# Batch 0 of a three-block kernel: the low part of transposed P by a matmul, normalization and the low part of q on POOL

## The chip, the cores and the metric

One core of a Trainium2 chip runs the whole program. The metric is device time in microseconds for one execution; the time before is the median of three runs. The engines are PE (matmul), DVE (vector), ACT (scalar), POOL (GpSimd) and SP, which here only issues transfers. Each engine works through its own instructions in order.

## The reference

Three blocks follow one another: attention that keeps only scores near the row's maximum, a gated feed-forward block, and a block with a two-dimensional Fourier transform and a second feed-forward part. The change touches the attention of the first of four batches.

```
q, k, v: (4, 8, 576, 64);  x: (4, 576, 512)
scores = q @ k.T / 8
keep   = scores >= rowmax - tau
attn   = exp(scores - rowmax) where kept, else 0
attn   = attn / (rowsum + 1e-9)
x      = attn @ v                      # heads side by side: 512
xk, xr = mixes of x with the row before it
x      = sigmoid(xr @ w_r) * (relu(xk @ w_k)**2 @ w_v)
u      = x + real(fft2(x))
out    = u + relu(layernorm(u) @ w_ch1) @ w_ch2
```

## The kernel before

All matmuls are to be nearly exact in fp32, but run on operands of type fp32r, which hold fewer bits. So each operand is split into a high part (a copy into fp32r, on ACT) and a low part (the value less the high part), and the products are added up in PSUM. Much of the work of DVE, ACT and POOL is this splitting.

Attention runs over 16 pairs of heads, 4 for each batch, and 9 steps for each pair: steps 0 to 3 and 5 to 8 take 128 rows of one head each, step 4 the 64 rows that remain of both heads. A step goes like this:

- `emit_scores` (line 212, and 226 for step 4): PE multiplies q with the high and low part of k, into PSUM tile "s".
- `emit_max` (252): DVE takes the row maximum; `emit_th` the threshold.
- `emit_exp` (263): ACT takes the exponential into SBUF tile "e" ("em" for step 4).
- `emit_select` (267): DVE zeroes what lies below the threshold and sums the rows; lines 626 and 630 make the reciprocal.
- the normalization: POOL multiplies the rows by it (`emit_norm`, 273), or ACT does (636), as the mask NA0 says step by step for batch 0.
- two steps later `emit_T` (320): PE transposes four 128 x 128 blocks into PSUM tile "t" (two buffers), a fifth one (340) for every second tile.
- its `out`: the transposed P is split into a high and a low part, tile "pt". With the mask SO0 set, ACT copies "t" to SBUF (331) and to the high part (332), and POOL subtracts (333). Otherwise ACT makes the high part and DVE subtracts (305, 306).
- `emit_av` (387, 389): PE multiplies with v, some steps later.

The heads' q and k are loaded by SP into one tile, "rawqk", of a pool with one buffer that v uses too. `conv_k` makes the high part of k on ACT (150) and the low part on POOL (151); `conv_q` makes the high part of q on ACT (157) and the low part on DVE (167), which scales and subtracts in one instruction. These conversions are emitted one pair ahead.

While batch 0 is in work, `weight_pieces` also converts weights for the feed-forward block, 20 pieces of 512 columns, with three DVE instructions on integers (67, 68, 69), a copy on ACT (72) and a subtraction on POOL (73). When all four pairs of a batch are done, the feed-forward block for it starts (line 413 and on), between the attention steps of the next batch. After attention follow the rest of the feed-forward block, the Fourier transform and the mixer.

The order of instructions on each engine is not written by hand: a scheduler puts them in order by priorities from the table `P` and by the times that it expects. The mask bits are the step's place in the pair: 239 is all steps but 4 and 8, 254 is steps 1 to 7. `pi < NPAIR` is batch 0.

Of the kernel before, what the change touches and what calls it, by code (L numbers as in the profile page):

```python
# [9 lines left out]
F32 = mybir.dt.float32  # L10
F32R = mybir.dt.float32r
I32 = mybir.dt.int32
ALU = mybir.AluOpType
AF = mybir.ActivationFunctionType
# [6 lines left out]
HS = S // 2  # L21
NPAIR = H // 2
P = dict(PRI=100, SR=1.0, CR=2, ORD=0, PF=0, CB=0, XT=0, XL=0, K2=0, FE=0, FE3=0, MU=0, WP=256, C1=2, RB=4, BB=2, FT=4, A0=[7, 8], A1=[11, 12], B0=[7, 8], B1=[11, 12], PT4=1, OR0='', XH=0, SP0=0, CA=1.48, CN=2.22, QS=1, pF=100, pM=100, pN=100, pT=100, pO=100, pE=100, pS=100, pA=0, pX=0, NA=0, LT=2, WS=3, WR=1, CC=3.0, BN=2, OR='FATXOESBI', TM=8, SO=0, SO0=0, AO=0, AO0=0, QS0=0, XD=0, TH=0, SM=0, SM0=0, N0=34, qF=100, qM=100, qN=100, qT=100, qO=100, qE=100, qS=100, qA=100, qX=30, RQ=[0,0,0,0,0,0,0,0], XN=0, QN=36, AVR=0, LX=2, WD=0, WP2=512, E3=1, NA0=0, W0=0, XD2=0, PO=0, WP1=512, IN=[0,1,2,2,4,5,6,7])
P.update({'pX': 100, 'CR': 3, 'pA': 100, 'OR': 'FTBXOAESI', 'PF': 300, 'pE': 0, 'pO': 500, 'QS': 2, 'WS': 0, 'FE3': 2, 'pF': 0, 'A0': [7, 9], 'C1': 3, 'BN': 2, 'K2': 0, 'WR': 0.9, 'FT': 2, 'MU': 0, 'SR': 0.6, 'XT': 0, 'SO0': 239, 'XL': 3, 'QS0': 2, 'FE': 2, 'CB': 2, 'AO0': 8, 'IN': [0, 0, 2, 2, 4, 5, 6, 6], 'pN': 30, 'pM': 0, 'A1': [11, 12], 'AVR': 1, 'NA0': 254, 'N0': 30, 'PT4': 0, 'WD': 1, 'qN': 0, 'qS': 500, 'qT': 150, 'QN': 37, 'qE': 0, 'qO': 30, 'B0': [7, 10], 'qX': 60, 'qM': 500, 'E3': 1, 'WP1': 512, 'qF': 300, 'OR0': 'FTBXEOASI', 'B1': [10, 13], 'TH': 4, 'AO': 4, 'qA': 30, 'pS': 300, 'SO': 16, 'RQ': [0, 0, 0, 0, 0, 0, 0, 0]})
PRI = P['PRI']


# [1 line left out]
def tile_kernel(ctx: ExitStack, tc: tile.TileContext, a):  # L29
    nc = tc.nc  # L30
    pe, dve, act, pool, sp = nc.tensor, nc.vector, nc.scalar, nc.gpsimd, nc.sync
# [8 lines left out]
    ident = const.tile([128, 128], F32, name="ident")  # L40
    small = const.tile([128, 46], F32, name="small")
    mus, cons, stats = small[:, 0:16], small[:, 16:19], small[:, 19:46]
# [111 lines left out]
    def conv_q(pi, j):  # L154
        raw, kh, kl = heads[pi, j]
        q = at.tile([128, 640], F32R, tag="q", bufs=3, name="q")
        act.activation(q, raw[:, 0:640], AF.Copy, scale=cons[:, 0:1])
        ql, x = q[64:128], raw[64:128, 0:640]
        qs = P['QS' if pi >= NPAIR else 'QS0'] if pi + j else 2
        if qs == 0:  # L160
            pool.tensor_scalar(x, x, cons[64:128, 0:1], 1.0, op0=ALU.mult, op1=ALU.mult)
            pool.tensor_tensor(ql, x, ql.bitcast(F32), op=ALU.subtract)
        elif qs == 1:
            dve.tensor_scalar(x, x, cons[64:128, 0:1], None, op0=ALU.mult)
            pool.tensor_tensor(ql, x, ql.bitcast(F32), op=ALU.subtract)
        else:
            dve.scalar_tensor_tensor(ql, x, cons[64:128, 0:1], ql.bitcast(F32), op0=ALU.mult, op1=ALU.subtract)  # L167
        heads[pi, j] = (q, kh, kl)
# [25 lines left out]
    def step_of(n):  # L194
        pi, s = divmod(n, 9)
        return pi, ORDER[s]
# [93 lines left out]
    def unit(pi, j, half):  # L290
        if (pi, j, half) not in ptu:
            m = 4 * pi + 2 * half + j
            if P['PT4'] and m % 4 == 3 and m < 4 * NPAIR - 2:
                ptu[pi, j, half] = stage.tile([128, 2, 4, HS], F32R, tag="pt", name="pt4")
            else:
                ptu[pi, j, half] = at.tile([128, 2, 4, HS], F32R, tag="pt", bufs=3, name="pt")
        return ptu[pi, j, half]

    def rem_unit(pi, half):
        if (pi, half) not in ptr:  # L300
            ptr[pi, half] = at.tile([128, 2, HS], F32R, tag="ptr", bufs=2, name="ptr")
        return ptr[pi, half]

    def split_out(hi, lo, src):
        act.activation(hi, src, AF.Copy)  # L305
        dve.tensor_tensor(lo, src, hi.bitcast(F32), op=ALU.subtract)  # L306

    def emit_T(n):
        if not 0 <= n < NSTEP:
            return []  # L310
        pi, tl = step_of(n)
        if tl is None:
            return emit_Tmix(pi, 0)
        j, i = tl
        e = et[pi, i]
        o = 640 if j else 0
        half, sl = i // 2, slice(128 * (i % 2), 128 * (i % 2) + 128)
        t = pst.tile([128, 4, 128], F32, tag="t", name="t")
        for k in range(4):
            pe.transpose(t[:, k, :], e[:, o + 128 * k:o + 128 * (k + 1)], ident)  # L320

        def out():
            u = unit(pi, j, half)
            hi, lo = u[:, 0, :, sl], u[:, 1, :, sl]
            if pi < NPAIR and P['SP0'] >> (n % 9) & 1:
                act.activation(hi, t, AF.Copy)
                pe.matmul(t.rearrange("p k x -> p (k x)"), nid, hi, start=False, stop=True, skip_group_check=True)
                act.activation(lo, t, AF.Copy)
            elif P['SO' if pi >= NPAIR else 'SO0'] >> (n % 9) & 1:
                f = e[:, o:o + 512].rearrange("p (k x) -> p k x", k=4)  # L330
                act.activation(f, t, AF.Copy)
                act.activation(hi, t, AF.Copy)
                pool.tensor_tensor(lo, f, hi.bitcast(F32), op=ALU.subtract)
            else:
                split_out(hi, lo, t)

        todo = [out]
        if j == 1:
            t2 = pst.tile([128, 128], F32, tag="t", name="t2")
            pe.transpose(t2, e[:, 512:640], ident)  # L340

            def out2():
                r = rem_unit(pi, half)
                split_out(r[:, 0, sl], r[:, 1, sl], t2)

            todo.append(out2)
        return todo

    def emit_Tmix(pi, half):
        e = em[pi * 9 + 4]  # L350
        t = pst.tile([128, 4, 2, 2, 32], F32, tag="t", name="tm")
        for k in range(4):
            pe.transpose(t[:, k].rearrange("p a b c -> p (a b c)"), e[:, 128 * k:128 * (k + 1)], ident)
        sl = slice(256, HS)

        def out():
            for j in range(2):
                u = unit(pi, j, half)
                split_out(u[:, 0, :, sl], u[:, 1, :, sl], t[:, :, j, half, :])

        def out2():
            t2 = pst.tile([128, 32], F32, tag="t", name="tm2")
            for j in range(2):
                c = 64 * j + 32 * half
                pe.matmul(t2[64 * j:64 * j + 64], e[:, 512:576], ident[:, c:c + 32], start=True, stop=True)
            r = rem_unit(pi, half)
            split_out(r[:, 0, sl], r[:, 1, sl], t2)

        return [out, out2]
# [195 lines left out]
    dve.tensor_scalar(cons[:, 1:2], tau, -1.0, 0.0, op0=ALU.mult, op1=ALU.min)  # L565
    conv_k(0, 0)
    conv_q(0, 0)
    load_head(0, 1)
    sp.dma_start(ident, a["ident"])
    sp.dma_start(mus[:, 0:4], a["mu_k"])  # L570
    sp.dma_start(mus[:, 4:8], a["mu_r"])
    dve.tensor_scalar(mus[:, 8:16], mus[:, 0:8], -1.0, 1.0, op0=ALU.mult, op1=ALU.add)
    conv_k(0, 1)
    conv_q(0, 1)
    load_v(0)
    conv_v(0)
# [18 lines left out]
    for n in range(P['LX']):  # L595
# [3 lines left out]
    state = dict(stream=None, credit=0.0, w=0.0, s=P['LX'] + 1, m=P['LX'], e=P['LX'])  # L599
    IN = (  # L600
        (load_head, 1, (0,)), (conv_k, 1, (0,)), (conv_q, 1, (0,)), (load_v, 0, ()), (conv_v, 0, ()),
        (load_head, 1, (1,)), (conv_k, 1, (1,)), (conv_q, 1, (1,)),
    )
# [47 lines left out]
    def do_T(n, pi, s):  # L651
        with hp('pT'):
            outs_of[n] = emit_T(n - P['LT'])
# [554 lines left out]
```

## Time and profile before

| what | value |
|---|---|
| median of 3 runs | 1136.56 us (1135.72 to 1139.6) |
| the profiled execution, its own time | 1139.89 us |
| its span in the trace | 1138.1 us |
| busy PE / DVE / ACT / POOL | 1038.4 / 806.7 / 588.9 / 483.8 us |
| mean granted share of the PE clock | 0.969 |

The busy times are over the whole span, in which the first stage (attention of batch 0) is a small part; the rows below are taken from that stage. "A <- B" means that instruction A stood idle until B released it. Matmuls overlap each other in the pipeline, so a busy PE is not PE at its peak.

### The profile page before, as it was taken

To read this page: it belongs to the slowest core of one execution; us is meant where nothing else is said; L and a number is where in the kernel's file an instruction comes from. 1 tells how busy PE (TensorE), PEld (TensorE's weight loads), DVE (VectorE), ACT (ScalarE), POOL (GpSimd) and SP (SyncE) were. 2 spreads that over 40 slices of the span, in tenths; PEclk is the share of its full clock that TensorE was granted. 3 is DMA by queue.
4 is the path that set the end of the run, shared out by engine and by line. 5 is a ranking of instruction groups with operands and counts; after the bars stand their busy time and mean duration, and the time that the engine had idled before them with its cause. 6 is when DMAs were issued, how large, how long until landed. Compare 5 with 4: busy or idle time off the path is not lost.

```text
span 1138.1 us, 19981 instructions
## 1 busy us (share of the span) xinstructions
PE 1038.4 (91%) x7109; PEld 960.0 (84%) x7109; DVE 806.7 (71%) x2093; ACT 588.9 (52%) x1396; POOL 483.8 (43%) x633
## 2 busy tenths in 40 slices
PE   4566769999999999999999997999999999999998
PEld 3555649999988999889988986889999999999997
DVE  7999889889889798897865677975553959322222
ACT  5787777768586685866736564433331212111111
POOL 4556576746467364673634253530001636100000
PEclk9888789999999999999999998999999999999999
DMA  5333321101112011121016255663442546223231
GB/s 171 111 119 96 98 73 56 48 30 54 55 56 76 30 47 56 56 76 32 24 65 159 93 162 178 199 205 120 153 143 90 185 158 190 98 93 109 77 111 56
DMA packets 40395, 114.07 MB, mean 100 GB/s; under 512 B 6191, under 2 KB 6612, under 8 KB 40296
## 3 DMA queue, kind: packets, MB, share of 16 engines
q1 hardware_dynamic: 27200, 74.57, 20.4%
q0 software_dynamic: 10400, 33.50, 9.1%
q10 hardware_dynamic: 2696, 4.73, 1.2%
q8 instruction: 56, 0.92, 0.3%
q14 instruction: 43, 0.35, 0.1%
HBM read 84.45 MB, written 28.32 MB: 99 GB/s over the span
## 4 chain that ended last, share of the span: by engine, by line
PE 65%; DVE 16%; ACT 7%; DMA 6%; issue 4%; POOL 2%; SPq 0%; DVEq 0%; ACTq 0%; POOLq 0%
PE c1ps L969 6%; PE c1ps L971 6%; PE c1ps L970 6%; PE c2ps L984 6%; PE c2ps L982 6%; PE c2ps L983 6%; PE av L387 3%; PE s L212 3%; DVE q L167 3%; DMA rawqk<-in_qk 2%; PE t L320 2%; DVE small L252 2%; PE kps L413 2%; DVE e L267 2%; PE kps L415 2%
## 5 line engine op out<-in xcount | busy, mean ns | idle before, releaser
L975 DVE SCALAR_TENSOR_TENSOR hl<-c1ps,hh 128x256 fp32r<-128x256 f32 x144 | 60.4, 421 | 161.2 <-ACT hh L974 160.6
L974 ACT ACTIVATE hh<-c1ps 128x256 fp32r<-128x256 f32 x144 | 54.3, 379 | 205.7 <-PE c1ps L971 205.6
L252 DVE TENSOR_REDUCE small<-s 128x1 f32<-128x576 f32 x144 | 107.3, 750 | 15.7 <-PE s L212 14.7
L1007 POOL DMA_DIRECT2D ud<-u x54 | 29.5, 546 | 194.2 <-DVE u L1006 138.4
L267 DVE SCALAR_TENSOR_TENSOR e<-s,small,e 128x576 f32<-128x576 f32 x128 | 102.4, 811 | 7.3 <-ACT e L263 5.6
L273 POOL TENSOR_SCALAR e<-e,small 128x576 f32<-128x576 f32 x104 | 82.3, 797 | 46.4 <-DVE small L630 35.4
L263 ACT ACTIVATE e<-s,small 128x576 f32<-128x576 f32 x128 | 92.6, 742 | 14.4 <-DVE small L252 13.4
L212 PE MATMUL s<-kh,q 128*128 128x288 f32 x256 | 65.4, 340 | 29.8 <-DVE q L167 13.7
L320 PE MATMUL t<-ident,e 128*128 128x128 f32 x512 | 81.2, 290 | 7.9 <-DVE ptr L306 2.9
L969 PE MATMUL c1ps<-ut,cA 128*128 128x256 f32 x288 | 82.5, 286 | 2.2 <-ACT ut L960 1.5
L970 PE MATMUL c1ps<-ut,cA 128*128 128x256 f32 x288 | 82.0, 285 | 0.0
L523 PE MATMUL vps<-k,wv 128*128 128x288 f32 x256 | 76.7, 302 | 5.4 <-DVE tg L529 4.6
L971 PE MATMUL c1ps<-ut,cA 128*128 128x256 f32 x288 | 81.6, 283 | 0.0
L971 PE MATMUL c1ps<-ut,cB 128*128 128x256 f32 x288 | 81.0, 281 | 0.0
L969 PE MATMUL c1ps<-ut,cB 128*128 128x256 f32 x288 | 80.9, 281 | 0.0
L970 PE MATMUL c1ps<-ut,cB 128*128 128x256 f32 x288 | 80.7, 280 | 0.0
L485 POOL TENSOR_TENSOR k<-relu,k 128x288 fp32r<-128x288 f32 x64 | 54.1, 847 | 60.6 <-ACT k L483 59.7
L306 DVE TENSOR_TENSOR pt<-t,pt 128x512 fp32r<-128x512 f32 x100 | 67.8, 684 | 16.4 <-ACT pt L305 15.7
L413 PE MATMUL kps<-xh,wk 128*128 128x288 f32 x256 | 78.3, 306 | 0.8 <-ACT relu L470 0.4
L387 PE MATMUL av<-pt,v 128*128 128x288 f32 x408 | 71.3, 308 | 8.1 <-ACT pt L305 3.8
L414 PE MATMUL kps<-xl,wk 128*128 128x288 f32 x256 | 75.8, 296 | 0.0
L415 PE MATMUL kps<-xh,wk 128*128 128x288 f32 x256 | 75.6, 296 | 0.0
(240 smaller groups left out, 3552.8 us busy)
## 6 DMA issues: line engine op xcount, KB each, us to landing
rawqk<-in_qk SPq DMA_DIRECT2D x32, 608.0 KB
u<-ud SPq DMA_DIRECT2D x36, 512.0 KB
wraw<-in_w_ch POOLq DMA_DIRECT2D x64, 256.0 KB, 3.3
ud<-u POOLq DMA_DIRECT2D x54, 256.0 KB, 2.5
rawv<-in_v SPq DMA_DIRECT2D x16, 288.0 KB
un<-ud SPq DMA_DIRECT2D x18, 256.0 KB
out<-u SPq DMA_DIRECT2D x18, 256.0 KB
wraw<-in_w_k SPq DMA_DIRECT2D x8, 512.0 KB
```

What stands on the lines that cost most here:

```text
L212: pe.matmul(ps[:, h, 0:HS], q[:, c:c + 128], kk[:, h * HS:(h + 1) * HS], start=(x == 0), stop=(x == 1),)
L252: dve.tensor_reduce(st[:, 0:1], sps[n][:, :, 0:HS], axis=AX.XY, op=ALU.max, negate=True)
L263: act.activation(two(eview(n)), sps[n][:, :, 0:HS], AF.Exp, bias=st[:, 0:1])
L267: dve.scalar_tensor_tensor(e, sps[n][:, :, 0:HS], st[:, 1:2], e, op0=ALU.is_ge, op1=ALU.mult, accum_out=st[:, 2:3])
L273: pool.tensor_scalar(e, e, st[:, 2:3], 1.0, op0=ALU.mult, op1=ALU.mult)
L320: pe.transpose(t[:, k, :], e[:, o + 128 * k:o + 128 * (k + 1)], ident)
L387: pe.matmul(ps, v[:, 4 * j + k, :], u[:, x, k, :], start=(k == 0 and x == 0), stop=False)
L413: pe.matmul(ps, wh, x[0][:, k, :], start=(k == 0), stop=False)
L415: pe.matmul(ps, wl, x[0][:, k, :], start=False, stop=(k == nk - 1))
L969: pe.matmul(ps, wh, ut[0][:, k, :], start=(k == 0), stop=False)
L970: pe.matmul(ps, wh, ut[1][:, k, :], start=False, stop=False)
L971: pe.matmul(ps, wl, ut[0][:, k, :], start=False, stop=(k == 3))
```

## The change

For batch 0 alone, three switches are set anew. SP0 takes the steps that SO0 had: ACT makes the high part, PE adds minus the high part to the tile "t" in PSUM (a matmul with minus the identity), and ACT copies what is left as the low part. NA0 = 0 gives all normalizations to POOL. QS0 = 3 lets ACT scale q in place and POOL subtract, for all heads of batch 0 but the first. The tile `nid` with minus the identity is made once on ACT. For all batches, the four transposes of a tile are written as one group of matmuls, with the start flag on the first and the stop flag on the last.

```diff
-P.update({... 'SO0': 239, ... 'QS0': 2, ... 'NA0': 254, ...})
+P.update({... 'SP0': 239, 'SO0': 0, ... 'QS0': 3, ... 'NA0': 0, ...})
...
         if qs == 0:
             pool.tensor_scalar(x, x, cons[64:128, 0:1], 1.0, op0=ALU.mult, op1=ALU.mult)
             pool.tensor_tensor(ql, x, ql.bitcast(F32), op=ALU.subtract)
+        elif qs == 3:
+            act.activation(x, x, AF.Copy, scale=cons[64:128, 0:1])
+            pool.tensor_tensor(ql, x, ql.bitcast(F32), op=ALU.subtract)
...
         for k in range(4):
-            pe.transpose(t[:, k, :], e[:, o + 128 * k:o + 128 * (k + 1)], ident)
+            pe.matmul(
+                t[:, k, :], e[:, o + 128 * k:o + 128 * (k + 1)], ident,
+                start=(k == 0), stop=(k == 3), is_transpose=True, skip_group_check=True,
+            )
```

The two branches of `out` that the masks choose between were in the kernel before:

```python
if pi < NPAIR and P['SP0'] >> (n % 9) & 1:
    act.activation(hi, t, AF.Copy)
    pe.matmul(t.rearrange("p k x -> p (k x)"), nid, hi, start=False, stop=True, skip_group_check=True)
    act.activation(lo, t, AF.Copy)
elif P['SO' if pi >= NPAIR else 'SO0'] >> (n % 9) & 1:
    f = e[:, o:o + 512].rearrange("p (k x) -> p k x", k=4)
    act.activation(f, t, AF.Copy)
    act.activation(hi, t, AF.Copy)
    pool.tensor_tensor(lo, f, hi.bitcast(F32), op=ALU.subtract)
```

## Rows read from the trace of the kernel before

**Rows 1.** Stretches: us; length, busy PE, PEld, DVE, ACT, POOL; PEclk, DMA, GB/s.

```profile
20.00:60.00 40.00, 25.38 (x128) 22.64 (x128) 38.00 (x98) 30.84 (x60) 22.49 (x19) 0.87 0.37 112
60.00:100.00 40.00, 27.05 (x157) 23.45 (x156) 37.49 (x91) 31.33 (x67) 24.68 (x22) 0.79 0.38 114
100.00:140.00 40.00, 26.64 (x148) 23.52 (x146) 35.28 (x94) 31.36 (x65) 25.51 (x23) 0.79 0.34 103
140.00:175.00 35.00, 23.09 (x123) 19.42 (x122) 30.81 (x74) 24.28 (x52) 26.85 (x28) 0.80 0.20 62
175.00:220.00 45.00, 43.02 (x328) 41.23 (x327) 40.02 (x118) 36.96 (x89) 29.99 (x40) 1.00 0.16 50
220.00:600.00 380.00, 365.09 (x2786) 350.78 (x2786) 318.50 (x895) 258.30 (x618) 213.31 (x286) 1.00 0.17 53
```

**Rows 2.** DVE's waits on other compute engines, 0 to 175 us: total, times, longest.

```profile
...
DVE small L252 <- PE s L212: 2.9, 6, 0.9
...
```

**Rows 3.** The chain that ended last, 20 to 175 us: its head, by line.

```profile
by line: issue 13.1%; DVE small L252 10.7%; DVE e L267 8.9%; DVE wbits L68 6.8%; DVE wbits L69 6.0%; DVE wbits L67 5.9%; PE avs L387 5.3%; DVE q L167 5.0%; PE s L212 3.4%; PE t L320 2.9%; DMA wraw<-in_w_v 2.7%; PE s L226 2.4%; POOL kl L151 
...
```

**Rows 4.** DVE's groups, 0 to 175 us: busy us, mean ns, idle before.

```profile
...
L68 DVE SCALAR_TENSOR_TENSOR wbits<-wraw,wbits 128x512 int32<-128x512 int32 x20 | 19.7, 986 | 0.1
L69 DVE SCALAR_TENSOR_TENSOR wbits<-wraw,wbits 128x512 int32<-128x512 int32 x20 | 19.0, 948 | 0.1
L67 DVE TENSOR_SCALAR wbits<-wraw 128x512 int32<-128x512 int32 x20 | 15.4, 771 | 2.4 <-POOL wr L73 0.8 <-POOL wk L73 0.8 <-DMA wraw<-in_w_v 0.6
...
```

**Rows 5.** Single lines, 0 to 175 us: ns min/median/max, first and last start.

```profile
L67 DVE TENSOR_SCALAR wbits<-wraw x20: 406/427/1500, 7.6 to 163.0; 128x512 int32<-128x512 int32 x20
...
L68 DVE SCALAR_TENSOR_TENSOR wbits<-wraw,wbits x20: 675/989/1878, 8.0 to 163.8; 128x512 int32<-128x512 int32 x20
...
L69 DVE SCALAR_TENSOR_TENSOR wbits<-wraw,wbits x20: 672/692/1634, 8.8 to 165.6; 128x512 int32<-128x512 int32 x20
...
L252 DVE TENSOR_REDUCE small<-s x41: 730/747/759, 9.4 to 174.3; 128x1 f32<-128x576 f32 x41
...
```

**Rows 6.** Stretches of line 167 alone: length, busy DVE; PEclk, DMA, GB/s.

```profile
10.00:115.00 105.00, 8.07 (x7) 0.85 0.38 116
115.00:175.00 60.00, 3.89 (x3) 0.77 0.26 77
...
```

**Rows 7.** ACT's groups, 0 to 175 us.

```profile
...
L636 ACT ACTIVATE e<-e,small 128x576 f32<-128x576 f32 x24 | 18.4, 774 | 6.1 <-DVE small L630 5.9
L332 ACT ACTIVATE pt<-t 128x512 fp32r<-128x512 f32 x28 | 16.7, 598 | 0.0
...
L157 ACT ACTIVATE q<-rawqk,small 128x640 fp32r<-128x640 f32 x11 | 9.0, 818 | 0.0
...
```

**Rows 8.** POOL's groups, 0 to 175 us.

```profile
L333 POOL TENSOR_TENSOR pt<-e,pt 128x512 fp32r<-128x512 f32 x28 | 39.1, 1397 | 22.4 <-ACT pt L332 14.4 <-PE t L320 5.6 <-issue 2.3
L151 POOL TENSOR_TENSOR kl<-rawqk,kh 128x576 fp32r<-128x576 f32 x10 | 15.9, 1593 | 7.6 <-ACT kh L150 4.2 <-PE tm L365 3.4
...
L273 POOL TENSOR_SCALAR e<-e,small 128x576 f32<-128x576 f32 x11 | 10.3, 939 | 6.9 <-DVE small L630 5.8 <-DVE ptr L306 1.1
...
```

**Rows 9.** Timeline at the start: start us, us, instruction, idle before it.

```profile
15.05 0.85 PE L212 MATMUL s<-kh,q 128*128 128x288 f32 x2 [6.13 <-DVE q L167]
```

**Rows 10.** What SP's queue waited for, 0 to 175 us.

```profile
...
SPq L143 <- DVE q L167: 25.6, 6, 7.1
...
```

**Rows 11.** What engines waited for, 20 to 175 us.

```profile
...
ACT kh L150 <- DMA rawqk<-in_qk: 3.8, 5, 1.8
...
```

**Rows 12.** Single lines: 982 over the span, 387 from 20 to 175 us.

```profile
L982 PE MATMUL c2ps<-cA,hh x144: 389/389/501, 703.2 to 1035.3; 128*128 128x512 f32 x144
...
L387 PE MATMUL avs<-pt,v x104: 290/442/608, 40.9 to 151.5; 128*128 128x288 f32 x104
...
```

**Rows 13.** PE's waits, 20 to 175 us.

```profile
...
PE tm L353 <- ACT pt L332: 7.3, 4, 3.0
...
PE t L340 <- ACT pt L332: 3.8, 4, 2.0
...
```

More of the change, by code (lines that the diff above doesn't have):

```diff
@@ L23 @@
 P = dict(PRI=100, SR=1.0, CR=2, ORD=0, PF=0, CB=0, XT=0, XL=0, K2=0, FE=0, FE3=0, MU=0, WP=256, C1=2, RB=4, BB=2, FT=4, A0=[7, 8], A1=[11, 12], B0=[7, 8], B1=[11, 12], PT4=1, OR0='', XH=0, SP0=0, CA=1.48, CN=2.22, QS=1, pF=100, pM=100, pN=100, pT=100, pO=100, pE=100, pS=100, pA=0, pX=0, NA=0, LT=2, WS=3, WR=1, CC=3.0, BN=2, OR='FATXOESBI', TM=8, SO=0, SO0=0, AO=0, AO0=0, QS0=0, XD=0, TH=0, SM=0, SM0=0, N0=34, qF=100, qM=100, qN=100, qT=100, qO=100, qE=100, qS=100, qA=100, qX=30, RQ=[0,0,0,0,0,0,0,0], XN=0, QN=36, AVR=0, LX=2, WD=0, WP2=512, E3=1, NA0=0, W0=0, XD2=0, PO=0, WP1=512, IN=[0,1,2,2,4,5,6,7])
-P.update({'pX': 100, 'CR': 3, 'pA': 100, 'OR': 'FTBXOAESI', 'PF': 300, 'pE': 0, 'pO': 500, 'QS': 2, 'WS': 0, 'FE3': 2, 'pF': 0, 'A0': [7, 9], 'C1': 3, 'BN': 2, 'K2': 0, 'WR': 0.9, 'FT': 2, 'MU': 0, 'SR': 0.6, 'XT': 0, 'SO0': 239, 'XL': 3, 'QS0': 2, 'FE': 2, 'CB': 2, 'AO0': 8, 'IN': [0, 0, 2, 2, 4, 5, 6, 6], 'pN': 30, 'pM': 0, 'A1': [11, 12], 'AVR': 1, 'NA0': 254, 'N0': 30, 'PT4': 0, 'WD': 1, 'qN': 0, 'qS': 500, 'qT': 150, 'QN': 37, 'qE': 0, 'qO': 30, 'B0': [7, 10], 'qX': 60, 'qM': 500, 'E3': 1, 'WP1': 512, 'qF': 300, 'OR0': 'FTBXEOASI', 'B1': [10, 13], 'TH': 4, 'AO': 4, 'qA': 30, 'pS': 300, 'SO': 16, 'RQ': [0, 0, 0, 0, 0, 0, 0, 0]})
+P.update({'pX': 100, 'CR': 3, 'pA': 100, 'OR': 'FTBXOAESI', 'PF': 300, 'pE': 0, 'pO': 500, 'QS': 2, 'WS': 0, 'FE3': 2, 'pF': 0, 'A0': [7, 9], 'C1': 3, 'BN': 2, 'K2': 0, 'WR': 0.9, 'FT': 2, 'MU': 0, 'SR': 0.6, 'XT': 0, 'SP0': 239, 'SO0': 0, 'XL': 3, 'QS0': 3, 'FE': 2, 'CB': 2, 'AO0': 8, 'IN': [0, 0, 2, 2, 4, 5, 6, 6], 'pN': 30, 'pM': 0, 'A1': [11, 12], 'AVR': 1, 'NA0': 0, 'N0': 30, 'PT4': 0, 'WD': 1, 'qN': 0, 'qS': 500, 'qT': 150, 'QN': 37, 'qE': 0, 'qO': 30, 'B0': [7, 10], 'qX': 60, 'qM': 500, 'E3': 1, 'WP1': 512, 'qF': 300, 'OR0': 'FTBXEOASI', 'B1': [10, 13], 'TH': 4, 'AO': 4, 'qA': 30, 'pS': 300, 'SO': 16, 'RQ': [0, 0, 0, 0, 0, 0, 0, 0]})
 PRI = P['PRI']
```

## Prediction

> **What bounds the kernel now.** I read the table of stretches first. Up to about 175 us only attention of batch 0 and the conversion of the first weights run; there DVE works 38.0 of 40, 37.5 of 40, 35.3 of 40 and 30.8 of 35 us, together 141.6 of the 155 us from 20 to 175 (91%), while PE has 102.2 us, ACT 117.8 and POOL 99.5. From 175 on PE takes over: 43.0 of 45 us, then 365 of 380 (96%) [rows 1]. So the kernel has a first stage paced by DVE and a long rest paced by PE, and what the first stage loses or gains moves the rest as a block.
>
> Next I asked who DVE waits for. The largest entry for another compute engine is a row maximum waiting for its scores, 2.9 us in six waits over 175 us [rows 2]: DVE is fed and is short of time. The chain of waits agrees: the DVE lines named in its head (252, 267, 68, 69, 67, 167) make 43.3% of 20 to 175 us, the PE lines 387, 212, 320 and 226 together 14.0% [rows 3]. Line 167, the low part of q, has 5.0% of it, which is 7.8 us.
>
> Then the durations. The weight conversion on DVE (lines 67 to 69, operands all in SBUF) takes 771, 986 and 948 ns on average [rows 4], but 406, 675 and 672 ns at best and up to 1878; the row maximum, which reads PSUM, always takes 730 to 759 [rows 5]. The spread belongs to DVE instructions that read SBUF alone, and the engine next to them there is POOL. The loss is (365 + 311 + 276) ns x 20 = 19.0 us of DVE time.
>
> **The change part by part.** Three switches act on the four pairs of batch 0 only; the flags of the transposes change everywhere.
>
> *Low part of q (QS0 2 to 3).* Of eight heads in batch 0 the first keeps its way, seven change. DVE loses line 167 for them: 8.07 us, seven instructions between 10 and 115 us [rows 6]. ACT gains seven scalings of 64 x 640; the row of the same width is line 157, 818 ns [rows 7], so +5.7 us. POOL gains seven subtractions; its 576-wide one (line 151) takes 1593 ns [rows 8], so 1770 ns by width, +12.4 us. The first of the seven stands on the start: PE starts on its scores at 15.05 us, after 6.13 us of waiting for that DVE instruction [rows 9]. ACT has to scale and POOL to subtract instead, after POOL's low part of k; I count 0 to +1.5 us there, because the DVE slot that was before it goes too, and take 0.
>
> Whoever reads the raw tile last sets when the next load starts: there is one buffer, and SP's queue stands for line 167 in 25.6 us of waits before loads of q and k [rows 10]. Behind a waiting load on SP stand the next loads of weights and v. The last reader is now a POOL subtraction, up to 1.8 us later. The cover is the distance of two or more steps between load and scores; today ACT stands only 3.8 us for these loads, in five waits [rows 11]. Price if that cover is gone: 7 x 1.8 = 12 us of ACT time, of an engine with 37 us idle. I take 0.
>
> *Normalizing on POOL (NA0 254 to 0).* 28 of the 36 steps leave ACT: 28 x 774 ns = -21.7 us [rows 7]. POOL gains 28 x 939 ns (line 273, its mean in this stretch) = +26.3 us [rows 8]. Nothing waits at once: the transposes of a step come two steps later.
>
> *Low part of transposed P (SO0 239 to 0, SP0 0 to 239).* 28 tiles. ACT keeps two passes over the tile (598 ns for one [rows 7]), only the second now follows a matmul. POOL loses 28 x 1397 ns = -39.1 us [rows 8]. PE gains 28 matmuls of 512 columns: 389 ns where the same shape runs today at full clock, and at most double, since the 288-column matmul of this stage ranges from 290 to 608 [rows 12]; +10.9 to +21.8 us, against 52.8 us of PE idle in 20 to 175. PE takes its instructions in order, so scores and attention-times-v queue behind a matmul that waits for ACT. The two PSUM tiles "t" are also held longer, by a matmul and a handoff; PE already stands for ACT's read of one, 7.3 us and 3.8 us in four waits each [rows 13]. Cover: DVE's own load, since scores are made more than one step ahead. I take 0 and keep the other end as a rival.
>
> *Flags of the transposes; the tile of minus identity.* Same four matmuls per tile, and readers needed the last one before too: 0. One 128 x 128 copy on ACT at the start, below the 598 ns of a 512-wide one: 0.
>
> *Sums for the first stage.* ACT 117.8 - 21.7 + 5.7 = 101.8. POOL 99.5 - 39.1 + 26.3 + 12.4 = 99.1, no change. PE 113 to 124. DVE 141.6 - 8.1 = 133.5 and still the fullest. What POOL does to DVE lies between two ends: if each us of POOL work costs DVE alike, nothing changes; if only two-input subtractions count, these fall by 26.7 of about 89 us (99.5 less the 10.3 of line 273), and of the 19.0 us lost 5.7 come back. Line 273 is itself no shorter for its single input by much (939 ns for 576 elements, 1397 for 512 with two inputs), so it occupies the same neighbourhood of DVE, and I stay near the first end: -1 us.
>
> The Trainium skill, SBUF — State Buffer, section "Who interferes with whom", says that a DVE instruction with two SBUF inputs and a GpSimd instruction that reads SBUF exclude one another, for a whole instruction, and that ACT never waits. The stretched rows agree with it. By that rule a POOL normalization blocks as a subtraction does, and the sum would be -8.1 without the -1.
>
> *What reaches the end.* DVE gives up 9.1 us. If all of it shortens the stage: -9.1. If only the share that line 167 has on the chain (7.8 of its 11.96 us up to 175 us, 65%) counts: 0.65 x 8.07 = -5.3. DVE is busy 91% of the stage; nearer to the first end, I take -8. The work after 175 us is unchanged and PE-paced, so it moves with it. Against the profiled execution: 1139.89 - 8 = 1131.9. That execution lies 3.3 us above the median, so the median becomes 1136.56 - 8 = 1128.5.
>
> **The rivals.** About 0.3%, 3.4 us, is what a measurement of this kernel tells from no change.
>
> *No change: the new work on POOL holds DVE up.* DVE's work on SBUF alone is 54.1 us in lines 67 to 69 [rows 4] and 8.1 in line 167, 62 of 142 us (44%). If the seven new subtractions hold DVE up for that share, 12.4 x 0.44 = 5.5 us come back, and 8.1 - 5.5 = 2.6 us of gain are left: 1134. For it: single conversions stretched to 1500 and 1878 ns. Against it: POOL's total does not rise, and the 39.1 us taken away held DVE up in the same way. The page Perfetto Trace Analysis of the Trainium skill, section "Optimizing Scalar/DVE Operations", warns of this: moving work between DVE and GpSimd might not help, since they share an SBUF port.
>
> *Slower: the round trip PE, ACT, PE, ACT paces the stage.* PE's idle of 52.8 us less 16 for the new matmuls is 36.5 us, less 8 if the stage shortens; so above about 1.0 us (28.5 / 28) of extra standing per tile PE, not DVE, sets the stage, and above 1.3 us (36.5 / 28) the kernel is slower than before. At the 1.8 us of today's mean wait of line 353 for ACT, each of 28 tiles would cost 50.4 us, 14 more than the idle: 1150. For it: PE's order, two tiles only, and a clock of 0.79 to 0.87. Against it: ACT gets 16 us lighter, so it reaches the high part sooner, and the new matmul can be placed later behind other PE work.
>
> *More than forecast.* The 5.7 us of stretch come back and everything counts: -8.1 - 5.7 = -13.8, 1123. For it: the waits of ACT and PE for one another also shrink as ACT is lighter. Against it: POOL keeps its total.
>
> **How the numbers follow.** Forecast (1126 to 1133, likeliest 1128.5): 0.50. More: 0.18. No change, 1133.1 to 1140: 0.18. Slower: 0.14. So faster 0.68, same 0.18, slower 0.14. The range 1121 to 1139 leaves about 0.05 below and 0.15 above. The likeliest case alone has 1126 to 1133.
>
> **What would show it.** Right: no line 167 on DVE for seven heads, DVE busy still about 90% up to the first feed-forward matmul, that matmul about 8 us before the 175 us of today, PE's windows after it as before, lines 67 to 69 at nearly the same means. Wrong: PE idle in front of the minus-identity matmul or of transposes growing beyond 1 us per tile; DVE waiting for scores for more than some us; lines 67 to 69 clearly longer or shorter; or a stage that shortens while the rest, reordered, gives it back. The last would break the step that carries the shift to the end one to one.

## Result and the profile after

The changed kernel takes 1145.56 us (median of seven runs, 1142.99 to 1152.37) where the kernel before, measured beside it, takes 1138.22 us: ratio 1.0076 with the interval 1.0057 to 1.0095. It is slower. The forecast was 1128.5 us, faster; the range 1121 to 1139 does not hold the result.

The profiled execution of the changed kernel has a span of 1143.4 us. Lines have moved: 167 is now 170, 252 is 255, 267 is 270, 273 is 276, 320 is 323, 353 is 359, 387 is 393, 413 is 419; 164 and 165 are the new scaling of q on ACT and subtraction on POOL, and 332, 333, 334 are the high part, the matmul with minus the identity and the low part. The stretches, with the columns of [rows 1]:

```profile
20.00:60.00 40.00, 25.75 (x121) 21.93 (x119) 35.20 (x96) 27.88 (x55) 28.48 (x26) 0.83 0.39 120
60.00:100.00 40.00, 29.46 (x153) 23.23 (x151) 31.92 (x90) 27.58 (x57) 23.34 (x24) 0.79 0.35 109
100.00:140.00 40.00, 30.60 (x164) 24.78 (x165) 34.61 (x94) 28.30 (x59) 22.21 (x24) 0.83 0.33 102
140.00:175.00 35.00, 26.72 (x162) 21.99 (x160) 26.96 (x76) 25.55 (x59) 19.31 (x25) 0.90 0.22 62
...
175.00:220.00 45.00, 40.94 (x278) 38.93 (x278) 37.20 (x107) 31.91 (x77) 29.49 (x39) 0.89 0.14 48
220.00:600.00 380.00, 363.09 (x2773) 348.96 (x2772) 317.48 (x892) 260.09 (x617) 213.23 (x282) 1.00 0.15 47
```

DVE did get lighter: 128.7 of the 155 us from 20 to 175, against 141.6 in [rows 1]. The stage did not get shorter by that: the first feed-forward matmul starts at 173.8 us, against 174.6 before, 0.8 us earlier for 12.9 us less DVE work. And from 175 to 220 us PE now has gaps and a lower granted clock (40.9 of 45 us, 0.89, against 43.0 and 1.00). In slices of 5 us:

```profile
175.00:180.00 5.00, 4.70 (x27) 4.46 (x26) 4.90 (x13) 2.74 (x6) 4.38 (x6) 0.66 0.27 109
...
185.00:190.00 5.00, 3.70 (x17) 3.49 (x16) 4.29 (x15) 2.58 (x8) 3.71 (x4) 0.57 0.36 126
```

Before, both slices were granted the full clock, with 41 and 33 matmuls where these have 27 and 17.

DVE's groups up to 175 us answer to [rows 4]; the last figure is idle time before:

```profile
L69 DVE SCALAR_TENSOR_TENSOR wbits<-wraw,wbits 128x512 int32<-128x512 int32 x20 | 20.1, 1003 | 0.2
L68 DVE SCALAR_TENSOR_TENSOR wbits<-wraw,wbits 128x512 int32<-128x512 int32 x20 | 17.0, 850 | 0.1
L67 DVE TENSOR_SCALAR wbits<-wraw 128x512 int32<-128x512 int32 x20 | 9.5, 473 | 10.0 <-POOL wk L73 8.7 <-POOL wr L73 0.9 <-POOL wv L73 0.2
...
L170 DVE SCALAR_TENSOR_TENSOR q<-rawqk,small,q 64x640 fp32r<-64x640 f32 x4 | 4.8, 1194 | 3.0 <-ACT q L157 3.0
```

The same sixty conversions take 46.6 us instead of 54.1, 7.5 us less; in line 67, whose waits for POOL grew in exchange, 5.9 of them. Where DVE stands now, beside [rows 2]:

```profile
DVE wbits L67 <- POOL wk L73: 8.7, 4, 3.6
DVE xt L402 <- ACT xt L401: 4.1, 6, 0.9
DVE small L255 <- PE s L215: 4.1, 8, 1.8
```

So much of DVE's relief became standing: in front of conversions whose buffer POOL still reads, and in front of ACT and PE. The chain of waits from 20 to 175 us, beside [rows 3]:

```profile
by line: DMA rawqk<-in_qk 13.4%; issue 7.9%; PE avs L393 6.7%; POOL v L192 6.0%; POOL e L276 4.9%; DVE e L270 3.9%; PE t L323 3.8%; ACT e L266 3.5%; DVE wbits L69 3.4%; ACT pt L332 3.3%; POOL q L165 3.2%; PE s L215 2.9%; DVE wbits L68 2.8%;
...
42.17 1.56 POOL q L165
43.75 3.86 DMA rawqk<-in_qk
...
115.90 1.55 POOL q L165
117.47 4.29 DMA rawqk<-in_qk
```

No engine has most of it. The largest item is the load of q and k, which twice starts right behind the new POOL subtraction. What was priced for POOL, ACT and PE:

```profile
L276 POOL TENSOR_SCALAR e<-e,small 128x576 f32<-128x576 f32 x35 | 30.6, 880 | 29.7 <-DVE small L636 25.3 <-DVE xt L404 2.0 <-PE t L346 1.5
...
L165 POOL TENSOR_TENSOR q<-rawqk,q 64x640 fp32r<-64x640 f32 x7 | 11.7, 1670 | 2.9 <-ACT rawqk L164 2.6
...
L276 POOL TENSOR_SCALAR em<-em,small 128x576 f32<-128x576 f32 x4 | 3.9, 966 | 1.3 <-DVE small L636 1.3
```

```profile
L332 ACT ACTIVATE pt<-t 128x512 fp32r<-128x512 f32 x28 | 16.6, 594 | 12.2 <-PE t L323 11.9
L334 ACT ACTIVATE pt<-t 128x512 fp32r<-128x512 f32 x28 | 15.8, 593 | 0.4 <-PE t L333 0.3
...
L164 ACT ACTIVATE rawqk<-rawqk,small 64x640 f32<-64x640 f32 x7 | 5.8, 823 | 0.2
```

```profile
L333 PE MATMUL t<-pt,nid 128*128 128x512 f32 x28 | 13.9, 504 | 6.8 <-ACT pt L332 6.8
```

POOL has 35 normalizations of "e" where [rows 8] had 11, and four of "em": the 28 have moved.

### The profile page after: what moved, and what is told of

Same layout as the page of the kernel before. It is cut to its first block, busy times and chain, and to the rows that moved or that the text cites. A ratio compares the mean times of both kernels' runs of the same rounds, so it can differ in the third digit from the quotient of the medians.

```text
span 1143.4 us, 20022 instructions
## 1 busy us (share of the span) xinstructions
PE 1050.6 (92%) x7137; PEld 965.2 (84%) x7137; DVE 794.6 (69%) x2086; ACT 577.7 (51%) x1376; POOL 480.6 (42%) x640
## 4 chain that ended last, share of the span: by engine, by line
PE 64%; DVE 12%; ACT 8%; DMA 8%; POOL 5%; issue 3%; SPq 0%; ACTq 0%; DVEq 0%; POOLq 0%
PE c1ps L975 5%; PE c2ps L989 5%; PE c2ps L988 5%; PE c1ps L977 5%; PE c2ps L990 5%; PE c1ps L976 5%; DMA rawqk<-in_qk 4%; PE av L393 3%; PE s L215 3%; PE t L323 3%; PE kps L419 2%; PE kps L420 2%; PE kps L421 2%; PE vps L529 2%; DVE q L170 2%
## 5 line engine op out<-in xcount | busy, mean ns | idle before, releaser
L276 POOL TENSOR_SCALAR e<-e,small 128x576 f32<-128x576 f32 x128 | 103.8, 816 | 65.5 <-DVE small L636 55.9
L419 PE MATMUL kps<-xh,wk 128*128 128x288 f32 x256 | 79.4, 311 | 3.1 <-DVE small L632 1.5
L421 PE MATMUL kps<-xh,wk 128*128 128x288 f32 x256 | 76.8, 300 | 0.0
```

What stands on the lines that cost most here:

```text
L276: pool.tensor_scalar(e, e, st[:, 2:3], 1.0, op0=ALU.mult, op1=ALU.mult)
L419: pe.matmul(ps, wh, x[0][:, k, :], start=(k == 0), stop=False)
L421: pe.matmul(ps, wl, x[0][:, k, :], start=False, stop=(k == nk - 1))
```

## Experiments

The change has four parts: **Q** (QS0 2 to 3), **N** (NA0 254 to 0), **S** (SO0 239 to SP0 239) and **F** (flags of the transposes). The expectations weigh six theories. T1: the raw tile of q and k is freed later, since its last reader is now a POOL subtraction behind an ACT scaling, and the next load waits. T2: POOL's queue is held by the normalizations. T3: the round trip between PE and ACT paces the stage. T4: the scheduler, seeing other times in the first stage, writes another order for what follows it, and that order is worse. T5: conversions wait for POOL's line 73 because "wbits" has one buffer. T6: not DVE's total but the hand-overs of an attention step pace the stage, and the conversions only fill DVE's gaps.

Each kernel was timed in five rounds beside the kernel before; ratios are to that kernel, with 95% intervals.

**One part alone, on the kernel before** (each with F):

```diff
-'SO0': 239, 'QS0': 2, 'NA0': 254
+'SO0': 239, 'QS0': 3, 'NA0': 254            # Q alone
+'SO0': 239, 'QS0': 2, 'NA0': 0              # N alone
+'SP0': 239, 'SO0': 0, 'QS0': 2, 'NA0': 254  # S alone
+'SO0': 239, 'QS0': 2, 'NA0': 254            # F alone
```

> Of the change, the low part of q by ACT and POOL (QS0 = 3) and the grouped transposes; normalization and low part of P as before. Theory T1 (the one raw tile is freed later and its loads pace the first stage): slower by about the whole 7 us, the chain of 20 to 175 us shows the load of rawqk with some 20 us as in the changed kernel (13.4%). T2 (norms on POOL) and T3 (the round trip of PE and ACT): not slower, 5 to 8 us faster than before, since DVE loses 8 us of line 167. T4 (no single switch, but the order that the scheduler makes at the passage to the feed-forward block): anywhere within 1%, with a first stage that ends as before or earlier.

> Of the change, all normalizations of batch 0 on POOL (NA0 = 0) and the grouped transposes; POOL keeps the subtraction of P, so it is the most loaded here. T2 (POOL's queue delays norms, and these the transposes): slower by 7 us or more, PE's waits for POOL's e growing. T1 and T3: within 0.3% of before, unless POOL with 26 us more in the first stage becomes the bound (99.5 + 26 = 126 of 155 us, not yet full). T4: within 1%, to either side.

> Of the change, the low part of P by the matmul with minus the identity (SP0 = 239, SO0 = 0) and the grouped transposes; q and normalization as before. T3 (PE stands for ACT's high part, tiles t are held longer): slower by 7 us or more, PE's waits for ACT's pt lines 10 us or more above before. T1 and T2: faster than before by 2 to 6 us, since POOL loses 39 us in the first stage and holds DVE up less. T4: within 1%, to either side.

> Of the change, the grouped flags of the transposes alone; all three switches as before. All theories: the same as before within 0.3%, since each tile has the same four matmuls. If it moves by more, the grouping itself changes the order that the scheduler makes, which speaks for T4.

Measured: Q alone 1147.48 us, 1.0096 [1.0075, 1.0117]; N alone 1152.62, 1.0130 [1.0109, 1.0152]; S alone 1137.53, 1.0003 [0.9990, 1.0016]; F alone 1138.22, 1.0003 [0.9992, 1.0013]. F is nothing, as priced. S is nothing although it takes 37 us from POOL (62.7 us busy from 20 to 175 instead of 99.5) and puts the 28 matmuls on PE: PE's waits for ACT's two passes, lines 332 and 334, are 19.4 us where those for line 332 were 11.7 before, but no round trip shows in the time, so T3 falls. N alone is as T2 expected: slower, with PE standing 6.2 us for normalizations of "e" on POOL where it was 0.5. Q, the part that was to bring the gain, costs about 11 us alone by the ratio (9.1 by the medians), although DVE is busy 5.6 us less up to the first feed-forward matmul (148.3 us against 153.9); that matmul comes at 181.1 us.

The chain of the kernel with F alone has a lesson of its own:

```profile
by line: PE avs L393 8.8%; issue 8.8%; DVE small L255 7.7%; DVE e L270 5.7%; PE t L323 5.7%; DVE q L170 5.7%; PE s L215 5.4%; DMA rawqk<-in_qk 5.1%; DVE wbits L68 3.8%; DVE wbits L69 3.8%; PE s L229 3.6%; ACT e L337 3.2%; ACT pt L338 3.1%; 
```

This kernel runs as long as the one before, yet the five DVE lines named here make 26.7% (67 has at most 3.1%, as the items fall in size), where the six of [rows 3] made 43.3%. So the shares of one chain are no steady measure of what an engine's work is worth. That the chain picks one of several paths that are nearly as long is a likely reason, not a shown one. Nor are the sums of rows steady: with F alone POOL has the work it had before, and yet the sixty conversions take 47.1 us (lines 67 to 69: 12.1, 19.6, 15.4), not 54.1.

**All parts but one:**

```diff
-'SP0': 239, 'SO0': 0, 'QS0': 3, 'NA0': 0    # the changed kernel
+'SP0': 239, 'SO0': 0, 'QS0': 2, 'NA0': 0    # without Q
+'SP0': 239, 'SO0': 0, 'QS0': 3, 'NA0': 254  # without N
+'SO0': 239, 'QS0': 3, 'NA0': 0              # without S
```

> The changed kernel with the low part of q back on DVE (QS0 = 2). T1 (the raw tile is freed later by the POOL subtraction): the loss goes, 5 to 10 us faster than the changed kernel, the loads of rawqk leave the chain. T2 and T3: as slow as the changed kernel or 8 us slower still, since DVE gets its 8 us back. T4: within 1%, to either side.

> The changed kernel with normalization split between ACT and POOL as before (NA0 = 254). T2: 5 to 10 us faster than the changed kernel. T1 and T3: as slow as the changed kernel. T4: within 1%, to either side.

> The changed kernel with the low part of P as before (SO0 = 239, POOL subtracts). POOL then has 39 us more in the first stage, 138 of 155 us. T3: faster than the changed kernel by 5 us or more. T1 and T2: slower than the changed kernel, since a fuller POOL delays the subtraction that frees the raw tile, or the norms: 5 to 15 us slower. T4: within 1%, to either side.

Measured: without Q 1138.83 us, 1.0007 [0.9995, 1.0020]; without N 1154.61, 1.0151 [1.0127, 1.0174]; without S 1146.41, 1.0077 [1.0056, 1.0098]. Taking Q out returns the whole loss. Taking N out makes it worse, so T2 falls for the changed kernel. Without S POOL is busy 131.9 us from 20 to 175 instead of 93.3, and the time stays: T3 expected 5 us or more less, T1 and T2 expected 5 to 15 us more, and none came. The parts don't add up: Q, N and S alone sum to +2.3%, together they are +0.76%; N costs 1.3% alone and nothing beside S. Nor has Q one price: it adds 0.9% to F, 1.5% to S and 0.7% to S and N, but takes 0.5% from N (1.0077 against 1.0130).

**Raw tiles, and the order behind the first stage.** Two more raw tiles for pairs 1 to 3, for T1. For T4, the order in which the scheduler of one kernel had put all instructions emitted from attention step 38 on (the third step of batch 1) is imposed on the other, on every engine, by edges that fix the order and add no wait; the first stage stays as its own scheduler makes it.

```diff
-raw = at.tile([128, 1216], F32, tag="raw", name="rawqk")
+if 1 <= pi < NPAIR:
+    raw = stage.tile([128, 1216], F32, tag="raw2", bufs=2, name="rawqk")
+else:
+    raw = at.tile([128, 1216], F32, tag="raw", name="rawqk")
...
     tile_kernel(tc, args)
+    pin_orders(nc, tc)   # each instruction behind its predecessor in the other kernel's order
```

Changed kernel with the raw tiles; changed kernel with the later order of before; kernel before with the later order of the changed one; changed kernel with both:

> The changed kernel with two more raw tiles for the q and k of pairs 1 to 3, so that their loads need not wait for the last reader. T1: the loss goes, 5 to 10 us faster than the changed kernel, and the loads of rawqk leave the chain of the first stage. T2, T3: within 0.3% of the changed kernel. T4: within 1%, to either side.

> The changed kernel, whose instructions emitted from attention step 38 on (all that no switch touches) are held, engine by engine, in the order that they have in the kernel before. The first 38 steps are free. T4 (the loss is the order that the scheduler chose after the first stage): the loss goes, 1136 to 1140 us, 5 to 9 us faster than the changed kernel, with the first feed-forward matmul where the changed kernel has it. T1, T2, T3 (raw tile, POOL's queue, round trip in the first stage): 1143 to 1147, as the changed kernel.

> The kernel before, with its instructions from attention step 38 on held in the order that they have in the changed kernel. No switch is set. T4: 1142 to 1147 us, slower than before by 4 to 8 us although none of the change is in it. T1, T2, T3: 1136 to 1140, as before.

> The changed kernel with two more raw tiles for q and k of pairs 1 to 3, the rest from step 38 on in the order of before. What the raw tile costs within the first stage shows here without the noise of the later order. T1: faster than the one with the order alone (a_pinb) by 5 us or more, so below 1134 if T4 is right too. If the raw tile costs nothing: within 3 us of a_pinb.

Measured, in this order: 1142.61 us, 1.0044 [1.0026, 1.0062]; 1143.32, 1.0049 [1.0034, 1.0064]; 1147.30, 1.0089 [1.0073, 1.0104]; 1138.93, 1.0014 [1.0003, 1.0026]. The changed kernel with the later order of before, first feed-forward matmul and the stretch behind it:

```profile
L419 PE MATMUL kps<-xh,wk x24: 288/293/399, 178.0 to 198.2; 128*128 128x288 f32 x24
```

```profile
175.00:220.00 45.00, 42.92 (x318) 41.08 (x318) 39.15 (x114) 34.39 (x83) 31.05 (x44) 0.98 0.16 50
```

It begins the feed-forward block 4.2 us later than the changed kernel does, yet its span is 1.8 us shorter (1141.6 against 1143.4): some 6 us that the changed kernel loses behind its first stage are not lost with the order of before, and the clock is at 0.98. These starts and spans are of one execution each, and executions of one kernel differ by some 5 us (1135.22 to 1139.95 before). Conversely the order of the changed kernel costs the kernel before 0.89% with no switch set. That bounds T4 loosely, since an order made for one first stage meets another. Of the 0.89%, some 10 us, 3.6 us are there before the first feed-forward matmul, which comes at 178.2 us. In the changed kernel itself the order is worth 0.27% (1.0076 to 1.0049; the intervals overlap), and 0.30% with the raw tiles (1.0044 to 1.0014). So T4 is a part: with the order of before the changed kernel still takes 1143 us, where T4 alone expected 1136 to 1140. T1 falls short as well: the tiles bring 3 us in the changed kernel and 4.4 us with the order held, where it expected 5 or more.

**Two buffers for the conversions** (T5), with the later order of before:

```diff
-weight_pieces(a[src], whole(w), stage, P['WP1'], 0, late if src == "w_v" else None)
+weight_pieces(a[src], whole(w), stage, P['WP1'], 0, late if src == "w_v" else None, 2, 2)
```

> The changed kernel with two buffers for the DVE side of the weight conversion (tile wbits) in place of one, the rest from step 38 on in the order of before. T5: the DVE time that was given up went into waits of line 67 for POOL's line 73, which has the norms and the q subtractions in front of it (8.7 us in the changed kernel up to 175 us, 0.8 before on wk). T5: that wait goes and the kernel is 4 to 8 us faster than a_pinb. T1: within 3 us of a_pinb.

Measured: 1151.26 us, 1.0115 [1.0097, 1.0133], slower than with one buffer (1.0049). The waits of line 67 for POOL on "wk" did shrink, from 8.3 us to 2.0, and the time did not follow. T5 falls.

**The test of the main step:** the kernel before, with 19 of the 20 conversions of the first stage made of one DVE instruction instead of three, and its own later order held.

```diff
 dve.tensor_scalar(w, h, 3, 0x3FFFFFFF, op0=ALU.logical_shift_left, op1=ALU.bitwise_and)
-dve.scalar_tensor_tensor(w, h, -0x40000000, w, op0=ALU.bitwise_and, op1=ALU.bitwise_or)
-dve.scalar_tensor_tensor(w, l, 29, w, op0=ALU.logical_shift_right, op1=ALU.bitwise_or)
+if stage is not light:
+    dve.scalar_tensor_tensor(w, h, -0x40000000, w, op0=ALU.bitwise_and, op1=ALU.bitwise_or)
+    dve.scalar_tensor_tensor(w, l, 29, w, op0=ALU.logical_shift_right, op1=ALU.bitwise_or)
```

> The kernel before, in which the 19 weight conversions of the first stage leave out two of their three DVE instructions (lines 68 and 69), so the weights come out wrong; the rest from step 38 on in the order of before. DVE loses some 37 of its 155 us in 20 to 175 us. If DVE paces the first stage, as the prediction said: first feed-forward matmul 20 us or more earlier and a kernel of 1110 to 1120 us. T6 (the attention steps are paced by the loop through PE, ACT, DVE and POOL, and the conversions only fill DVE's gaps): less than 6 us earlier, 1132 to 1140.

Measured: 1133.78 us, 0.9955 [0.9938, 0.9971]. Its stretch from 20 to 175 us, its first feed-forward matmul, and what DVE waited for there:

```profile
20.00:175.00 155.00, 109.19 (x593) 95.11 (x594) 118.43 (x336) 121.80 (x255) 97.52 (x96) 0.75 0.31 99
```

```profile
L414 PE MATMUL kps<-xh,wk x32: 288/294/401, 168.3 to 193.8; 128*128 128x288 f32 x32
```

```profile
DVE small L253 <- PE s L213: 8.4, 8, 1.8
DVE xt L397 <- ACT xt L396: 7.1, 7, 2.0
DVE q L168 <- ACT q L158: 6.4, 5, 2.6
DVE e L268 <- ACT e L264: 5.2, 8, 1.5
```

DVE is busy 23.2 us less in this stretch (118.4 against 141.6), but the stretch now holds 6.7 us of the next stage, in which it is busy too. Up to the first feed-forward matmul, before and with the lighter conversions:

```profile
0.00:174.60 174.60, 107.19 (x567) 93.35 (x568) 153.90 (x379) 125.74 (x254) 107.22 (x100) 0.83 0.36 109
0.00:168.30 168.30, 108.11 (x566) 93.68 (x567) 121.98 (x340) 124.82 (x253) 100.45 (x99) 0.77 0.35 113
```

DVE has 31.9 us less to do (122.0 against 153.9), the stage ends 6.3 us earlier (168.3 against 174.6) and the kernel gains 5.1 us (0.45% of 1138.42). About a sixth of this relief of DVE arrives. At 118 of 155 us it stands for PE, then ACT, then ACT again. One run does not say whether each microsecond counts a sixth or the first ones count in full until something else sets the pace. Three other kernels, in which q stays on DVE as before, speak against the second:

| kernel | DVE busy up to the first feed-forward matmul, us | that matmul, us | ratio to before |
|---|---|---|---|
| before | 153.9 | 174.6 | 1 |
| F alone | 148.4 | 172.3 | 1.0003 |
| S alone | 142.5 | 171.2 | 1.0003 |
| without Q, later order of before | 146.0 | 170.4 | 0.9995 |

DVE is relieved by 5.5 to 11.4 us, about as much as was forecast, the feed-forward block begins 2.3 to 4.2 us earlier, and no time is gained. (S and N put work on other engines, F does not.) So DVE was full in large part because conversions were put into its gaps. That the steps hold each other up (T6) is what is left and fits these waits; no run shows it by itself. Two rivals for where the relief went stand untested: the granted clock, 0.75 from 20 to 175 us where it was 0.81, and the load of q and k, which has 9.0% of this kernel's chain.

The Trainium skill, Perfetto Trace Analysis, section "Identifying the Most-Contended Engine", takes the engine with the highest occupancy as the one to relieve first. At 91% DVE was that engine by far, and its relief by lighter conversions is the only edit here that gained; but 31.9 us off it gave 5.1, so the occupancy did not tell what a relief is worth.

**What is left of Q and the raw tiles,** all with the later order of before: the changed kernel without Q; the kernel before with the raw tiles; the changed kernel without Q, with the raw tiles. The edits are those above.

> Normalization on POOL and the low part of P by the matmul, but the low part of q on DVE as before; the rest from step 38 on in the order of before. T1 (the low part of q on POOL costs, through the raw tile): about 4 us faster than the same with it (1143.3), so 1136 to 1140. T4 beside it: 1 to 3 us faster than the same kernel with its own later order (1138.8).

> The kernel before with two more raw tiles for q and k of pairs 1 to 3 and its own later order. Control for T1: if the wait for the raw tile is a cost that the change brought, this is within 0.3% of before. If the one raw tile costs before as much as the changed kernel, this is 4 us faster than before, and the tile does not explain the loss.

> The kernel with normalization on POOL, the low part of P by the matmul, q on DVE, two more raw tiles, and the later order of before: the candidate for a version that beats both. T6: no faster than 0.3% below before, since neither DVE nor the tile paces the steps. T1 with DVE as the pace: 1130 to 1134.

Measured: 1137.48 us, 0.9995 [0.9982, 1.0008]; 1145.24, 1.0059 [1.0044, 1.0074]; 1138.64, 1.0002 [0.9991, 1.0013]. With S and N set and the later order held, this makes a table of four:

| ratio to before | one raw tile | two more |
|---|---|---|
| q's low part on DVE | 0.9995 [0.9982, 1.0008] | 1.0002 [0.9991, 1.0013] |
| q's low part on POOL (Q) | 1.0049 [1.0034, 1.0064] | 1.0014 [1.0003, 1.0026] |

Q costs 0.54% (about 6 us) with one tile and 0.12% with more; the tiles bring 0.35% with Q and nothing without. The first feed-forward matmul starts at 178.0 us with Q and at 170.4 without it (one tile each). This supports T1 for some two thirds of Q's price. It isn't clean: the same tiles on the kernel before cost 0.59%, where T1 expects nothing; another order of the first stage, which the scheduler also writes, is the likely reason, not a shown one. Nor does one row of the trace carry it: with q on DVE the load of q and k has 12.5% of the chain, with Q 10.3%, and ACT's line 150 stands 7.1 us for these loads from 20 to 175 us without Q and 5.8 with it.

## Why the prediction was wrong

**What failed: "a first stage paced by DVE".** Two steps hung on it: that the stage gives up what DVE gives up ("I take -8"; the lower end named was -5.3), and that everything put on ACT, POOL and PE is covered by DVE's load. The run with lighter conversions shows the first wrong by a factor: a sixth arrives. If line 167 counted as the conversions do, its 8.07 us would have been worth under 2 us, inside what can't be told from no change; the three kernels of the table show reliefs of about that size that gained nothing. The 91% was read rightly, but about a third of DVE's work was filler (54.1 us of conversions), and the small waits of [rows 2] were no evidence: an engine with other work in hand does not stand, whoever paces the loop. The rows before did not settle it. Of PE's 53.5 us of waits from 20 to 175 us, 38.5 were for DVE and 14.5 for ACT, which fits a DVE that paces and a loop through all engines alike.

**DVE's loss of line 167:** right in size (seven instructions gone; four of 4.8 us left up to 175 us). **Contention:** I took -1 us with a bound of -5.7; the conversions take 7.5 us less, beyond the bound. POOL's two-input subtractions fell by 39.1 - 11.7 = 27.4 us while one-input normalizations rose by 24.2 (30.6 + 3.9 - 10.3). But the 7.5 us can't be given to that: with F alone, where POOL's work is as before, the conversions take 7.0 us less too. And of the 7.5 us, 5.9 came in line 67, whose waits for POOL rose from 1.6 to 9.8 us; lines 68 and 69 fell by 1.6 of 38.7. The rule of the Trainium skill, SBUF — State Buffer, section "Who interferes with whom", lets a DVE instruction with two SBUF inputs, as lines 68 and 69 are, contend with a normalization as with a subtraction. These sums neither bear it out nor refute it. That the stretched rows agree with it holds for these two lines only: line 67 reads one input from SBUF and stretched as well, from 406 ns to 1500 [rows 5].

**The later release of the raw tile and the longer way of q, priced at 0:** Q's cost decided the sign, since without Q the kernel is as before. I named the bare price of the later release, 12 us, and covered it with ACT's few waits of [rows 11]. Those waits by which I priced it went from 3.8 us only to 6.3, and are as long in kernels without Q (6.0 with S alone), so it is not by them that Q costs. With Q the chain goes from the load over ACT's scaling (0.82 us) and POOL's subtraction (1.67) where it went over one DVE instruction (1.19): 1.3 us more for each of seven heads, 9 us in sum, against 6 us measured with the later order held and 11 alone. That this longer way is the rest of Q's price is argued, not shown. At the start, the second head's scores came at 17.05 us instead of 15.05; I had bounded that at +1.5 and taken 0:

```profile
15.43 1.12 PE L323 MATMUL t<-ident,e 128*128 128x128 f32 x4 [6.37 <-POOL e L276]
17.05 0.85 PE L215 MATMUL s<-kh,q 128*128 128x288 f32 x2 [0.50 <-POOL q L165]
```

Whether these 2 us reach the end isn't shown: with the raw tiles and the later order of before that start is at 19.46 us, in a faster kernel.

**Normalizing on POOL:** 24 x 880 ns + 4 x 966 ns = 25.0 us, where I had 26.3. POOL fell to 93.3 us where I had 99.1, and ACT to 109.3 where I had 101.8: the busy times of ACT's groups fell by 14.3 us in sum up to 175 us, near the 16.0 that I had priced, but ACT's own busy time, in which instructions that overlap count once, by 9.1. That normalizing on POOL is free is right beside S (1.0003 without it, 1.0007 with it) and beside Q (1.0096 and 1.0077); alone it costs 1.3%.

**Minus identity:** 13.9 us at 504 ns, inside 10.9 to 21.8, and PE's 6.8 us of waits there, in 15 times, are 0.24 us a tile, far from the 1.0 us from which I let PE decide. **The rival "slower"** had the right sign with the wrong mechanism. **Flags:** 0, right.

**"The work after 175 us is unchanged and PE-paced, so it moves with it"** failed too. In the table above the feed-forward block begins up to 4.2 us earlier and the end does not move. I had named the way: a stage whose rest, reordered, gives it back. Between the start of the feed-forward block (-0.8 us) and the end (+5.3 us of span), the changed kernel loses 6 us, with PE's gaps and granted clocks of 0.57 to 0.66; with the order of before most of that is gone, but the stage is longer. Of the 0.76%, Q accounts for all by the run without it; the split is about 0.3% by the later order and 0.4 to 0.5% by the rest, of which the raw tile takes most by the table of four.

**Open:** the order inside the first stage could not be held while a part was changed, and its shuffles are worth as much as the parts (0.59% from raw tiles that should do nothing). So T1's share has that uncertainty, and why N costs 1.3% alone and Q takes 0.5% from it was not taken apart. The kernel before was not run with its own later order held and nothing else changed; without Q holding it costs nothing (1.0007 free, 0.9995 held). No version that does all the work beat the kernel before beyond what can be told from no change.

## What to carry to other kernels

A full engine need not be the bound: first sort its busy time into steps of the loop and filler that can go anywhere, and count as gain only what leaves the path. A split that moves from one instruction on one engine to two on two engines is to be priced by its way from the load to the freed buffer too, not only by the load of the engines. Where a scheduler writes the order, an edit also draws a new order of everything behind it; hold that order fixed in an experiment before giving a difference under 1% to the edit itself, and read the rows of a kernel whose work is unchanged beside it before giving a moved row to the edit.

## What the hardware showed unexpectedly

The clock granted to PE from 20 to 175 us ran from 0.70 (N alone) and 0.72 (Q alone, and the kernel before with raw tiles) to 0.85 and 0.86 (without Q with the later order of before, S alone); these are mixtures of the levels 1.2 and 2.4 GHz. The kernels that were 0.9 to 1.5% slower had 0.70 to 0.78, but the fastest of all, with the lighter conversions, had 0.75, and the changed kernel 0.83: the clock of this stage does not order the kernels, and whether a low one makes a stage longer or a stage with more waits gets a low one can't be read from these runs. The 128-row, 512-column matmul took 393 ns at best, 497 in the middle and 795 at most in this stage, where [rows 12] had 389 at full clock.
